# Second-part matmul groups in four single PSUM banks, and a LayerNorm finished for two tiles at a time, in a gated linear attention and gMLP kernel

## The chip, the cores and the metric

The kernel runs on one core of one Trainium2 chip. The metric is the device time of one execution in microseconds, and the kernel before and the changed one are compared by the medians of several executions. The core has five engines that run their own instruction streams side by side: TensorE (PE, with the loading of weights shown apart as PEld), VectorE (DVE), ScalarE (ACT), GpSimd (POOL) and SyncE (SP), whose queue issues the loads and stores. Matmuls write to PSUM, which has eight banks of 128 x 512 float32 values here; DVE and ACT carry results from there to SBUF.

## The reference

The first part is a recurrence over 768 tokens for 4 batches and 8 heads of 48, the second a gated MLP with a spatial mixing over the tokens:

```python
for t in range(S):
    state = alpha[:, :, t, :, None] * state + np.einsum('bhd,bhe->bhde', k[:, :, t], v[:, :, t])
    y[:, :, t] = np.einsum('bhd,bhde->bhe', q[:, :, t], state)
...
x = y.transpose(0, 2, 1, 3).reshape(B, S, H * D)            # 4 x 768 x 384
h = np.maximum(x @ w_in, 0.0)                               # d_ff = 1024
u, v = h[..., :512], h[..., 512:]
v_n = (v - mean(v)) / np.sqrt(var(v) + 1e-06)               # over the last axis
v_s = np.einsum('ts,bsd->btd', w_spatial, v_n) + b_spatial[None, :, None]
return (u * v_s) @ w_out                                    # 4 x 768 x 384, float32
```

## The kernel before, in words

The tokens are cut into tiles of 128: six per batch, 24 in all, numbered 0 to 23. `first(i)` lists the work on tile i of the recurrence in its chunked form: four loads (`ac`, `kc`, `qc`, `vc`: alpha, k, q and v, 192 KB each, on SP's queue), `ln` and the running sum `cum` (ACT, PE), the exponentials `einv`, `ebc`, `eexp` (ACT), the scaled `kt` (POOL) and `qt` (DVE), their transposes `trk` and `trq` (PE) and the copies out of PSUM `evk` and `evq` (ACT or DVE), the scores `sc` (PE), the masking `m` (DVE, tile `ptm`), the state's update `upd`, `z`, `S`, `sb` (PE, DVE, POOL), the output `y` (PE), and the transposition of `y` into `xT` of the batch (`xs`, `xt`, `xe`).

The second part works by batch. `second_v` multiplies `xT` by the second half of `w_in`, two tiles at a time, ACT applies the `relu` (line 139) and DVE takes the statistics (`bn`, lines 476 and 477). When all six tiles of a batch have theirs, `rs` makes `rstd` (two small ACT instructions, lines 486 and 487) and six `vn` normalise (DVE, line 493). `second_u` makes the other half, `second_s` the spatial product (six matmuls for each half `th` of the tokens) with its evacuation on DVE (line 541, and the product with `u` on POOL, line 553; in the last batch one DVE instruction, line 536). `second_o` multiplies by `w_out`, copies to `o_sb` and stores two tiles at a time (line 579). All these matmuls stand in the log under the helper's line 435.

`group` gives each of these steps one tile `ps2` of two PSUM banks out of a pool of two, so four banks in all. Two banks more serve `cum`, `tp` and `y`, and two hold `pt0` and `pt1`, each for a tile's transposes and then for its scores.

The order of each engine's instructions is not that of the listing. Every step is an `Op` with a planned duration, the steps it depends on, and a number `prio`; `schedule()` takes again and again the step that can start first by its plan, the lower `prio` where two can start at the same time, and emits it. The engines then run in that order and wait for each other by semaphores. A `Ring` stands for a pool of buffers in that plan.

Of the kernel before, what the change touches and what calls it, by code (L numbers as in the profile page):

```python
# [9 lines left out]
FP32 = mybir.dt.float32  # L10
# [6 lines left out]
class Op:  # L17


    def __init__(self, eng, dur, emit, deps=(), prio=0.0, take=None, give=(), lat=0.13):  # L20
        self.eng = {eng: dur} if isinstance(eng, str) else dict(eng)
        self.emit, self.prio, self.take, self.lat = emit, prio, take, lat
        self.deps = [d for d in deps if d is not None]
        self.give = list(give)
        self.end = None


class Ring:
# [5 lines left out]
    def free_at(self):  # L34
        n = len(self.taken) - self.bufs
# [13 lines left out]
def schedule(ops):  # L49
# [3 lines left out]
    while todo:  # L53
        best = None
        for n, op in enumerate(todo):
# [3 lines left out]
            if op.take is not None:  # L59
                f = op.take.ring.free_at()  # L60
                if f is None:
                    continue
                ready = max(ready, f)
# [12 lines left out]
        if op.take is not None:  # L76
            op.take.ring.taken.append(op.take)
# [6 lines left out]
def kernel(  # L84
# [26 lines left out]
    N = B * NCH  # L111

    consts = ctx.enter_context(tc.tile_pool(name="consts", bufs=1))
    IO = 7
# [30 lines left out]
    ident = consts.tile([128, 128], BF16, name="ident")  # L145
    mask4 = consts.tile([128, 4, 128], BF16, name="mask4")
# [11 lines left out]
    kt_bufs = [consts.tile([128, HP, 2, 64], BF16, name=f"kt{i}") for i in range(NB)]  # L158
    sbd_bufs = [consts.tile([128, HP, 2 * D], BF16, name=f"sbd{i}") for i in range(NB)]

    def constants(_):
        for t in la_bufs[:1] + qt_bufs[:1] + kt_bufs[:1] + sbd_bufs + la_bufs[1:] + qt_bufs[1:] + kt_bufs[1:]:
# [4 lines left out]
        nc.vector.memset(mask4, 0.0)  # L167
        nc.gpsimd.memset(ut_ones, 0.0)
# [9 lines left out]

    ops = []
# [15 lines left out]
    rings = {"a": Ring(2), "p0": Ring(1), "p1": Ring(1), "p2": Ring(2)}  # L195
# [4 lines left out]
    def first(i):  # L200
# [6 lines left out]
        def load(name, src):  # L207
            def emit(_):
                t = st[name] = io_pool.tile([128, H, D], FP32, name=name)
# [3 lines left out]
        for name, src, user in (("ac", alpha, "ln"), ("kc", k, "kt"), ("qc", q, "qt"), ("vc", v, "vb")):  # L213
            op((name, i), "SP", 1.11, load(name, src), got((user, i - IO)) + got(("order", i)), prio=P, lat=2.0)

# [11 lines left out]
        op(("ln", i), "ACT", 0.41, ln, got(("ac", i), ("cum", i - NB)), prio=P + 1)  # L227

        def cum(_):
            cm = st["cum"] = pp_a.tile([128, 512], FP32, name="cum", tag="a")  # L230
            nc.tensor.matmul(out=cm[:, 0:DM], lhsT=ut_ones, rhs=la[:, :, :, 0:D], start=True, stop=True)  # L231
            if not last:
                for hp in range(HP):
                    nc.tensor.matmul(  # L234
                        out=cm[:, DM + hp:DM + hp + 1], lhsT=la[:, hp, :, :], rhs=ones_col,
                        start=True, stop=True)

        sl_c = Slot(rings["a"])
        op(("cum", i), "PE", 0.16 if last else 0.3, cum, got(("ln", i)), prio=P + 2, take=sl_c)
# [8 lines left out]
        def eexp(_):  # L248
            nc.scalar.activation(out=st["cv"], in_=st["cv"], func=AF.Exp)  # L249

        op(("eexp", i), "ACT", 0.38, eexp, got(("einv", i)), prio=P + 3.1, use=[sl_c])
# [12 lines left out]
        def qtf(_):  # L264
            nc.vector.tensor_mul(out=qt[:, :, :, 0:D], in0=quad(st["qc"]), in1=st["cv"])  # L265
# [388 lines left out]
```

## Time and profile before

| what | us |
|---|---|
| median of 3 runs | 178.77 |
| lowest and highest | 178.15, 179.4 |
| the profiled execution | 177.04 |
| its span, first to last instruction | 175.3 |

The page begins with the share of each engine, and then the span in 40 slices of 4.4 us: each digit is the busy share of a slice in tenths, PEclk the clock that TensorE was granted in tenths of the full one.

```profile
PE 143.1 (82%) x1412; PEld 88.5 (50%) x1412; DVE 119.2 (68%) x257; ACT 98.0 (56%) x202; POOL 81.3 (46%) x134
## 2 busy tenths in 40 slices
PE   0562859838978999999978999999999899798960
PEld 0451536527545566655655666656565545343430
DVE  7374568763798489898899789998894467514400
ACT  4341567737796445789897664797874037300031
POOL 2641547642543569957823579985410770000000
PEclk9999999996995699999999999999999999999997
DMA  6999999999999999913979989869600001500033
```

The DMA engines are full for some 17 slices, PE from about the tenth slice on. A busy PE here is the union of its matmuls' durations, which overlap in the pipeline: a lone matmul of 384 columns lasts 0.34 us by its row, while 24 in a row take 4.06 us.

### The profile page before, as it was taken

How to read it: one execution, taken by the hardware profiler on the slowest of the kernel's cores; microseconds unless marked ns; L12 is line 12 of the kernel's file. 1: busy time of each engine (PE TensorE's matmuls, PEld its weight loads, DVE VectorE, ACT ScalarE, POOL GpSimd, SP SyncE). 2: the span in 40 equal slices, each digit the busy share in tenths (PEclk: the TensorE clock that was granted, in tenths of full speed). 3: DMA queues.
4: the chain of work that ended last, by engine and by line, in shares of the span. 5: the costliest groups of instructions: out<-in, count | busy, mean ns of one | idle time of the engine just before them, and what ended most of it. 6: DMA issues, size and time to landing. Idle time of an engine off the chain costs nothing.

```text
span 175.3 us, 3842 instructions
## 1 busy us (share of the span) xinstructions
PE 143.1 (82%) x1412; PEld 88.5 (50%) x1412; DVE 119.2 (68%) x257; ACT 98.0 (56%) x202; POOL 81.3 (46%) x134
## 2 busy tenths in 40 slices
PE   0562859838978999999978999999999899798960
PEld 0451536527545566655655666656565545343430
DVE  7374568763798489898899789998894467514400
ACT  4341567737796445789897664797874037300031
POOL 2641547642543569957823579985410770000000
PEclk9999999996995699999999999999999999999997
DMA  6999999999999999913979989869600001500033
GB/s 123 203 183 179 224 193 204 196 209 236 215 187 202 220 222 189 215 38 138 229 168 227 225 159 221 178 132 253 157 0 4 0 2 63 207 0 4 0 144 126
DMA packets 104947, 26.60 MB, mean 152 GB/s; under 512 B 100128, under 2 KB 104480, under 8 KB 104928
## 3 DMA queue, kind: packets, MB, share of 16 engines
q1 hardware_dynamic: 103104, 23.60, 63.7%
q0 software_dynamic: 1824, 2.75, 8.6%
q8 instruction: 11, 0.18, 0.4%
q14 instruction: 8, 0.07, 0.1%
HBM read 23.99 MB, written 4.72 MB: 164 GB/s over the span
## 4 chain that ended last, share of the span: by engine, by line
PE 46%; SPq 15%; DMA 13%; DVE 10%; ACT 10%; issue 3%; POOL 2%; ACTq 0%; POOLq 0%; DVEq 0%
PE ps L435 32%; SPq L210 15%; DMA ac<-in_alpha_dram 10%; PE pt L281 4%; DMA out_dram<-o_sb 3%; PE pt L344 2%; ACT o_sb L133 2%; DVE ptm L354 2%; PE y L390 2%; ACT v_sb L139 2%; DVE vsb L541 2%; DVE gT L536 2%; PE cum L231 2%; DVE stats L476 1%; PE tp L302 1%
## 5 line engine op out<-in xcount | busy, mean ns | idle before, releaser
L435 PE MATMUL ps<-w_spT,vn 128*128 128x384 bf16 x192 | 38.1, 338 | 1.0 <-DVE vsb L541 0.8
L354 DVE TENSOR_TENSOR ptm<-pt,mask 128x512 bf16<-128x512 f32 x48 | 30.8, 684 | 5.6 <-PE pt L344 5.1
L260 POOL TENSOR_TENSOR kt<-kc,binv 128x384 bf16<-128x384 f32 x24 | 21.9, 913 | 16.4 <-ACT bc L255 11.8
L553 POOL TENSOR_TENSOR gT<-vsb,uT 128x768 bf16<-128x768 f32 x12 | 19.6, 1642 | 13.0 <-DVE vsb L541 12.8
L435 PEld LDWEIGHTS <-vn 128*128 128x128 bf16 x192 | 17.6, 100 | 14.6 <-issue 5.9
L435 PE MATMUL ps<-xT,w_in_sb 128*128 128x384 bf16 x96 | 19.4, 326 | 2.7 <-ACT xT L133 1.0
L139 ACT ACTIVATE v_sb<-ps 128x1024 bf16<-128x1024 f32 x12 | 12.3, 1029 | 14.7 <-PE ps L435 14.6
L328 POOL TENSOR_TENSOR state<-state,bc 128x192 f32<-128x192 f32 x20 | 10.3, 513 | 21.7 <-DVE state L319 14.8
L133 ACT COPY o_sb<-ps 128x768 f32<-128x768 f32 x12 | 9.6, 806 | 18.8 <-PE ps L435 15.5
L435 PE MATMUL ps<-w_in_sb,xT 128*128 128x512 bf16 x72 | 19.1, 389 | 0.1
L265 DVE TENSOR_TENSOR qt<-qc,cum 128x384 bf16<-128x384 f32 x24 | 13.2, 549 | 8.4 <-ACT cum L249 4.8
L476 DVE BATCH_NORM_STATS2 stats<-v_sb 128x6 f32<-128x512 bf16 x24 | 16.3, 677 | 3.6 <-ACT v_sb L139 3.5
L225 ACT ACTIVATE la<-ac 128x384 bf16<-128x384 f32 x24 | 12.6, 524 | 10.7 <-DMA ac<-in_alpha_dram 10.7
L435 PE MATMUL ps<-w_out_sb,gT 128*128 128x384 bf16 x96 | 17.7, 325 | 0.8 <-DVE gT L536 0.3
L244 ACT ACTIVATE binv<-cum 128x384 bf16<-128x384 f32 x24 | 11.8, 492 | 11.7 <-PE cum L234 9.5
L133 ACT CAST x_sb<-y 128x384 bf16<-128x384 f32 x24 | 11.6, 483 | 7.7 <-PE y L371 7.7
L135 DVE COPY qkT<-pt 128x512 bf16<-128x512 bf16 x27 | 11.2, 421 | 6.7 <-PE pt L281 6.6
L271 POOL CAST vb<-vc 128x384 bf16<-128x384 f32 x24 | 12.1, 504 | 6.9 <-DMA vc<-in_v_dram 3.5
L231 PE MATMUL cum<-la,ut_ones 128*128 128x384 bf16 x24 | 8.6, 357 | 7.5 <-ACT la L225 6.8
L541 DVE TENSOR_TENSOR vsb<-ps,bsp_bc 128x768 f32<-128x768 f32 x12 | 11.4, 955 | 4.1 <-PE ps L435 3.9
L319 DVE TENSOR_TENSOR state<-tp,state 64x192 f32<-64x192 f32 x32 | 11.3, 353 | 3.6 <-PE tp L302 3.1
L133 ACT COPY qkT<-pt 128x512 bf16<-128x512 bf16 x21 | 12.4, 591 | 1.7 <-PE pt L281 1.6
(63 smaller groups left out, 243.7 us busy)
## 6 DMA issues: line engine op xcount, KB each, us to landing
ac<-in_alpha_dram SPq DMA_DIRECT2D x24, 192.0 KB, 3.8
kc<-in_k_dram SPq DMA_DIRECT2D x24, 192.0 KB, 3.9
qc<-in_q_dram SPq DMA_DIRECT2D x24, 192.0 KB, 3.7
vc<-in_v_dram SPq DMA_DIRECT2D x24, 192.0 KB, 3.7
out_dram<-o_sb SPq DMA_DIRECT2D x12, 384.0 KB, 2.5
wsp_nat<-in_moe_w_spatial_dram POOLq DMA_DIRECT2D x1, 1152.0 KB, 11.2
w_in_sb<-in_moe_w_in_dram POOLq DMA_DIRECT2D x1, 768.0 KB, 8.7
w_out_sb<-in_moe_w_out_dram POOLq DMA_DIRECT2D x1, 384.0 KB, 6.8
```

The lines of the kernel that those rows point to most:

```text
L133: nc.scalar.copy(out=out, in_=in_)
L139: nc.scalar.activation(out=out, in_=in_, func=AF.Relu)
L210: nc.sync.dma_start(out=t, in_=src[b, :, t0:t0 + C, :].rearrange("h s d -> s h d"))
L225: nc.scalar.activation(out=la[:, :, :, 0:D], in_=quad(st["ac"]), func=AF.Ln)
L231: nc.tensor.matmul(out=cm[:, 0:DM], lhsT=ut_ones, rhs=la[:, :, :, 0:D], start=True, stop=True)
L260: nc.gpsimd.tensor_mul(out=kt[:, :, :, 0:D], in0=quad(st["kc"]), in1=st["binv"])
L265: nc.vector.tensor_mul(out=qt[:, :, :, 0:D], in0=quad(st["qc"]), in1=st["cv"])
L354: nc.vector.tensor_tensor(out=st["ptm"][:, s], in0=st[f"pt{s}"], in1=mask4, op=ALU.mult)
L435: return lambda ps: nc.tensor.matmul(out=out(ps), lhsT=lhsT(), rhs=rhs(), start=start, stop=stop)
L476: nc.vector.bn_stats(out=stats, in_=d["v_sb"][:, tt, :])
L541: nc.vector.tensor_tensor(out=hold["vs"], in0=ps[:, :, 0:TH], in1=bsp_bc, op=ALU.add)
L553: nc.gpsimd.tensor_tensor(out=bt[b]["gT"][:, dsl, :].rearrange("p (a t) -> p a t", a=2), in0=hold["vs"], in1=bt[b]["uT"][:, dsl, :].rearra ...
```

## The change

Five things change, and the first two move the most instructions.

1. Second-part groups take one bank in place of two, from a pool of four (`pp_2`, ring `p2`). Each `v` group is now one tile, each `u` group one of four feature tiles, each `s` group one half of the tokens for one feature tile, each `o` group one tile. There are twice as many groups and evacuations, each of half the width; the matmuls are the same. `second_o` of a tile needs only the gated half that holds it, and `o_sb` has four buffers of half the size, with 24 stores in place of 12.
2. `second_ln` is gone: after every second tile, `second_v` lists `rs` and two `vn` for that pair. An `s` group comes in two pieces, the first with four token tiles and the second with two, and each waits only for its own `vn` (`pdeps`).
3. Every evacuation of a group gets `prio` 5.0 and every `rs` 6.0, so they precede all work of tiles 1 and later where both could start.
4. The scores no longer reuse the banks of the transposes: `pt` is one pool of two, from which each transposition and each half of the scores takes a bank when it needs it. `qkT` is split into `qT` and `kT`.
5. The loads of alpha and q get 4 buffers, those of k and v 6, where all had 7.

A second way to compute the first tiles (`fold`, with tokens interleaved in pairs) is in the code too, but `FOLD = 0` keeps it from being listed; only its constant tiles (`le_pair`, `lt_pair`, `le_tok`, and two alpha buffers) are filled at the start.

```diff
-    IO = 7
+    IO = 6
+    IO2 = 3
+    IO3 = 4
...
-    outp = ctx.enter_context(tc.tile_pool(name="outp", bufs=2))
+    outp = ctx.enter_context(tc.tile_pool(name="outp", bufs=4))
-    pp_p = ctx.enter_context(tc.tile_pool(name="pp_p", bufs=1, space=bass.MemoryType.PSUM))
-    pp_2 = ctx.enter_context(tc.tile_pool(name="pp_2", bufs=2, space=bass.MemoryType.PSUM))
+    pp_p = ctx.enter_context(tc.tile_pool(name="pp_p", bufs=2, space=bass.MemoryType.PSUM))
+    pp_2 = ctx.enter_context(tc.tile_pool(name="pp_2", bufs=4, space=bass.MemoryType.PSUM))
...
-        for t in la_bufs[:1] + qt_bufs[:1] + kt_bufs[:1] + sbd_bufs + la_bufs[1:] + qt_bufs[1:] + kt_bufs[1:]:
+        for t in la2_bufs[:1] + qt_bufs[:2] + kt_bufs + la2_bufs[1:] + sbd_bufs + qt_bufs[2:] + la_bufs:
             nc.vector.memset(t, 0.0)
...
+        nc.gpsimd.memset(le_tok, 0.0)
+        for ci in range(2):
+            nc.gpsimd.affine_select(
+                out=le_tok[64 * ci:64 * ci + 64], in_=le_tok[64 * ci:64 * ci + 64], compare_op=ALU.is_gt, fill=1.0,
+                base=0, channel_multiplier=2, pattern=[[1, 2], [-1, 128]],
+            )
+        for t, base in ((le_pair, 0), (lt_pair, 1)):
...
         nc.gpsimd.memset(ut_ones, 0.0)
...
-    rings = {"a": Ring(2), "p0": Ring(1), "p1": Ring(1), "p2": Ring(2)}
+    rings = {"a": Ring(2), "p": Ring(2), "p2": Ring(4)}
...
-        op(("sc", i), "PE", 0.4, sc, got(("evq", i), ("evk", i)), prio=P + 7, use=[sl0, sl1])
+        sl0, sl1 = Slot(rings["p"]), Slot(rings["p"])
+        qk = got(("evq", i0, 0), ("evq", i0, 1)) if fold else got(("evq", i))
+        op(("sc", i), "PE", 0.4, sc, qk + got(("evk", i)), prio=P + 7, take=[sl0, sl1])
...
-                    hold["ps"] = pp_2.tile([128, 2, 512], FP32, name="ps2")
+                    hold["ps"] = pp_2.tile([128, 512], FP32, name="ps2")
...
-        return op(key, eng, dur, lambda e: evac(e, hold["ps"]), [prev] + list(edeps), prio=prio, use=[sl])
+        return op(key, eng, dur, lambda e: evac(e, hold["ps"]), [prev] + list(edeps), prio=5.0, use=[sl])
...
-        op(("rs", b), "ACT", 0.45, rs, [made[("bn", b, t)] for t in range(NT)], prio=Q)
+        op(("rs", b, t0), "ACT", 0.45, rs, got(("bn", b, t0), ("bn", b, tt)), prio=6.0)
...
+        pdeps = [[made[x] for t in tt for x in (("vn", b, t), ("we", t))] for tt in ((0, 1, 2, 3), (4, 5))]
...
-        op(("st", b, tp), "SP", 1.11, store, got(("o", b, tp)), prio=-1.0, lat=2.0)
+            nc.sync.dma_start(out=out[b, tt * 128:(tt + 1) * 128, :], in_=hold["o"])
+        op(("st", b, tt), "SP", 0.56, store, got(("o", b, tt)), prio=-1.0, lat=2.0)
```

Three places show how the order moves. The first is where batch 0 ends and the scores of tile 7 are masked. On DVE before, between the masking of tile 6 and that of tile 7 (`ptm` with two score banks each):

```order
L354 TENSOR_TENSOR ptm<-pt_683,mask_87 128x512
L476 BN_STATS stats<-v_sb 128x6
L477 BN_AGGR mvs<-stats 128x2
L476 BN_STATS stats<-v_sb 128x6
L477 BN_AGGR mvs<-stats 128x2
L319 TENSOR_TENSOR state<-tp,state 64x192 x2
L493 TENSOR_SCALAR vn<-v_sb,mvs,rstd 128x512 x2
L354 TENSOR_TENSOR ptm<-pt_791,mask_87 128x512
L354 TENSOR_TENSOR ptm<-pt_811,mask_87 128x512
L493 TENSOR_SCALAR vn<-v_sb,mvs,rstd 128x512
L265 TENSOR_TENSOR qt_102<-qc,cum 128x8x48
L493 TENSOR_SCALAR vn<-v_sb,mvs,rstd 128x512 x3
```

The same place on DVE now:

```order
L477 TENSOR_TENSOR ptm<-pt,mask_90 128x512 x2
L594 BN_STATS stats<-v_sb 128x6
L595 BN_AGGR mvs<-stats 128x2
L144 TENSOR_SCALAR uT<-ps_869 128x384
L138 COPY kT<-pt 128x512
L438 TENSOR_TENSOR state<-tp,state 64x192
L612 TENSOR_SCALAR vn<-v_sb,mvs,rstd 128x512
L438 TENSOR_TENSOR state<-tp,state 64x192
L477 TENSOR_TENSOR ptm<-pt,mask_90 128x512 x2
L612 TENSOR_SCALAR vn<-v_sb,mvs,rstd 128x512
```

Two statistics and six `vn` around the masking have become one and two, and an evacuation of `u` and the copy of `kT` have come in. On PE before, from the last score of tile 7 to its `y` (rows left out are weight loads and repeats):

```order
L344 MATMUL pt_811<-qkT 128x128
...
L231 MATMUL cum<-la_99,ut_ones 128x384
...
L365 MATMUL y<-sbd_106,qkT 128x96
...
L371 MATMUL y<-vb,ptm 128x48
```

And on PE now:

```order
L465 MATMUL pt<-qT,kT 128x128
...
L513 MATMUL y<-ident,x_sb 128x128
...
L559 MATMUL ps_931<-w_spT,vn 128x384
...
L559 MATMUL ps_948<-w_spT,vn 128x384
...
L289 MATMUL cum<-la_102,ut_ones 128x384
...
L559 MATMUL ps_962<-w_spT,vn 128x384
...
L488 MATMUL y<-sbd_111,qT 128x96
...
L494 MATMUL y<-vb,ptm 128x48
```

Three pieces of the spatial product of batch 0 and a transposition of `x` now stand between the scores and `y`. The second place is the end, on ACT, from the last batch's first evacuations on. Before:

```order
L139 ACTIVATE uT<-ps_2547 128x2x384
L133 COPY o_sb<-ps_2558 128x768
L486 ACTIVATE rstd<-mvs,eps_tile 128x6
L487 ACTIVATE rstd<-rstd 128x6
L133 COPY o_sb<-ps_2574 128x768
L133 COPY o_sb<-ps_2589 128x768
L139 ACTIVATE uT<-ps_2617 128x2x384
L133 COPY o_sb<-ps_2697 128x768
L133 COPY o_sb<-ps_2702 128x768
L133 COPY o_sb<-ps_2718 128x768
```

Now:

```order
L142 ACTIVATE uT<-ps_2860 128x384
L142 ACTIVATE uT<-ps_2869 128x384
L605 ACTIVATE rstd<-mvs,eps_tile 128x2
L606 ACTIVATE rstd<-rstd 128x2
L136 COPY o_sb<-ps_2953 128x384
L136 COPY o_sb<-ps_2963 128x384
L136 COPY o_sb<-ps_2970 128x384
L136 COPY o_sb<-ps_2978 128x384
L136 COPY o_sb<-ps_2986 128x384
L136 COPY o_sb<-ps_2994 128x384
```

Copies of 384 columns stand where copies of 768 stood, and the last batch's `rstd` comes in three parts. The third place is SP's queue around the first stores. Before, where the loads of tile 15 begin:

```order
L210 DMA ac<-in_alpha_dram 128x8x48
L210 DMA kc<-in_k_dram 128x8x48
L579 DMA out_dram<-o_sb 128x2x384 x2
L210 DMA qc<-in_q_dram 128x8x48
L210 DMA vc<-in_v_dram 128x8x48
L210 DMA ac<-in_alpha_dram 128x8x48
L579 DMA out_dram<-o_sb 128x2x384
```

Now, where the loads of tile 12 begin:

```order
L231 DMA ac<-in_alpha_dram 128x8x48
L231 DMA kc<-in_k_dram 128x8x48
L684 DMA out_dram<-o_sb 128x384
L231 DMA qc<-in_q_dram 128x8x48
L231 DMA vc<-in_v_dram 128x8x48
L684 DMA out_dram<-o_sb 128x384 x2
L231 DMA ac<-in_alpha_dram 128x8x48
L684 DMA out_dram<-o_sb 128x384 x3
L231 DMA kc<-in_k_dram 128x8x48
```

The stores of batch 0 have moved three tiles ahead among the loads, and three of them stand between the alpha and the k of tile 13. The stores of batch 1, at tile 23 before, stand at tiles 19 and 20 now.

More of the change, by code (lines that the diff above doesn't have):

```diff
@@ L58, in schedule @@
             ready = max([d.end + d.lat for d in op.deps], default=0.0)
[L59 to L63, printed above, removed]
+            waits = [slot.ring.free_at(k) for k, slot in enumerate(op.take)]
+            if None in waits:
+                continue
+            ready = max([ready] + waits)
             for eng, dur in op.eng.items():
@@ L481, in second_ln, with bn @@
-    def second_ln(b):
-        Q = 1000.0 + 100 * b
+        group(("v", b, tt), mms, 0.22, got(("xe", b * NCH + tt), ("w_in",)), Q + tt, evac, {"ACT": 0.48}, None,
+              [made.get(("vn", b - 2, tt))], parts=1)
+        def bn(_):
+            d = bt[b]
+            stats = small.tile([128, 6], FP32, name="stats")
+            nc.vector.bn_stats(out=stats, in_=d["v_sb"][:, tt, :])
+            nc.vector.bn_aggr(out=d["mvs"][:, tt, :], in_=stats)
+        op(("bn", b, tt), "DVE", 0.85, bn, got(("v", b, tt)), prio=Q + 10)
@@ L575, in second_o @@
[L575 to L576 removed]
+            hold["o"] = outp.tile([128, DM], FP32, name="o_sb")
+            copy(eng, hold["o"], ps[:, 0:DM])
+        Q = 1000.0 + 100 * b + 30 + tt
+        group(("o", b, tt), mms, 0.165, [made[("g", b, x, tt // 3)] for x in range(NDS)] + got(("w_out",)), Q, evac,
+              {"ACT": 0.38, "DVE": 0.47}, None, [made.get(("st", b, tt - 4))], parts=1)
```

340 lines of the change are left out of this document (202 added, 138 removed).

## The prediction

> **What bounds the kernel now.** I read first the busy time by stage (columns: stretch, its length, then busy time and instructions of PE, PEld, DVE, ACT and POOL, then granted clock, DMA share and GB/s), then the chain of waits, then PE's own waits.
>
> ```profile
> 0.00:44.50 44.50, 26.43 (x304) 19.31 (x305) 27.52 (x67) 23.03 (x49) 20.96 (x43) 0.96 1.03 195
> 44.50:62.00 17.50, 15.27 (x154) 9.02 (x151) 13.32 (x31) 12.85 (x28) 7.76 (x15) 0.80 1.05 206
> 62.00:90.00 28.00, 27.30 (x317) 17.13 (x315) 24.70 (x53) 20.52 (x45) 20.54 (x31) 1.00 0.75 167
> 90.00:130.00 40.00, 37.85 (x432) 24.25 (x432) 35.80 (x78) 30.32 (x66) 25.58 (x41) 1.00 0.89 181
> 130.00:170.00 40.00, 36.24 (x217) 18.77 (x214) 17.83 (x32) 10.50 (x15) 6.49 (x4) 1.00 0.11 38
> ```
>
> ```profile
> 38.37 6.10 DMA ac<-in_alpha_dram
> ```
>
> Until 44.5 us the DMA engines are full (share 1.03) and PE works 26.4 of 44.5 us; the chain there ends in a load of alpha that lands at 44.5. The change moves the same bytes, so I let this stage stand: that alpha, of tile 7, lands at 44.5 in both kernels. Little second-part work can be pulled ahead of that moment, since it needs tiles that have not come; by the order, the new kernel has one group of three matmuls more behind it there.
>
> From 44.5 on PE is the bound (27.3 of 28.0, then 37.9 of 40.0 us). A gain there can only be PE time that is now waited for or run at a low clock. So the sum goes over PE's stands.
>
> **Term A, the LayerNorm of batch 0.** Before, all six `bn`, one `rs` and six `vn` of a batch come in one burst on DVE. The first fence is the timeline where it ends; the second gives windows (start and end, length, PE busy, instructions, granted clock, DMA share, GB/s).
>
> ```profile
> 50.71 0.93 DVE L493 TENSOR_SCALAR vn<-v_sb,mvs,rstd 128x512 bf16<-128x512 bf16 x2
> 51.67 1.29 DVE L354 TENSOR_TENSOR ptm<-pt,mask 128x512 bf16<-128x512 f32 x2
> 52.42 0.20 PE L371 MATMUL y<-vb,ptm 128*128 128x48 bf16 x1 [1.00 <-DVE ptm L354]
> 53.02 0.35 PE L371 MATMUL y<-vb,ptm 128*128 128x48 bf16 x7 [0.40 <-DVE ptm L354]
> 53.78 0.50 PE L281 MATMUL pt<-ident,kt 128*128 128x128 bf16 x3 [0.41 <-POOL kt L260]
> ```
>
> ```profile
> 36.00:38.00 2.00, 0.31 (x8) 1.00 1.25 238
> 40.00:42.00 2.00, 1.62 (x22) 0.50 1.16 308
> 52.00:54.00 2.00, 0.77 (x11) 0.82 0.72 139
> 54.00:60.00 6.00, 5.99 (x39) 0.50 1.10 218
> ```
>
> `y` of tile 7 needs the masked scores `ptm`; these stand on DVE behind two statistics and two `vn`. PE waits 1.00 + 0.40 + 0.41 = 1.8 us, and for the next 6 us its granted clock is 0.50: 6 x 0.5 = 3.0 us lost. After the change only `bn` of tile 5 and `vn` of tiles 4 and 5 are left at this place. DVE's row is not empty (an evacuation of `u` and of `k` now stand there too, some 1.3 us), so `ptm` is hardly earlier; what helps is PE's order. Three spatial matmul groups of batch 0 and the `x` transposes now stand between the scores and `y` of tile 7. Four tiles of vn are enough for them. These are some 2.3 us of PE work (the tail's full-clock rate is 0.163 us per matmul: 24 in 4.06 us, row below), which covers the 1.0 + 0.4 us. I take both parts: 1.8 and 3.0. Bounds: 0 and 1.8 for the wait, 0 or 3.0 for the clock.
>
> The earlier low clock (0.50 in 40 to 42) also came 2 to 4 us after a stretch in which PE did little (0.31 of 2.00 us). That supports tying the dip at 54 to the stand at 52. The Trainium skill (TensorE: Matmul & The Clock Gate, Part 1) says that the gate halves the clock after at least one idle window of about 3.4 us. The longest single stand here is 1.00 us, so by that rule the stand did not cause the dip, and the sum would be 172.8, the second case below. The trace agrees as to the two clocks, 1.00 and 0.50, and does not show the window's length.
>
> **Term B, the LayerNorm of batch 1.** The same burst, later:
>
> ```profile
> 91.74 0.65 PE L435 MATMUL ps<-xT,w_in_sb 128*128 128x384 bf16 x3 [0.77 <-ACT uT L139]
> 94.30 0.40 PE L281 MATMUL pt<-ident,qt 128*128 128x128 bf16 x4 [0.72 <-DVE qt L265]
> ```
>
> The first waits for a pair of banks to be emptied by one 768-wide `relu`, the second for DVE between two pieces of the `vn` burst. Both causes are split up by the change: 1.5 us, bounds 0 and 1.5.
>
> **Term C, the pairs of banks in the tail.** After tile 23 only second-part work is left, and PE waits for a pair to be emptied (the table of waits, 130 us to the end):
>
> ```profile
> PE ps L435 <- DVE gT L536: 1.1, 2, 0.8
> PE ps L435 <- ACT o_sb L133: 0.9, 2, 0.7
> PE ps L435 <- DVE vsb L541: 0.6, 1, 0.6
> PE ps L435 <- ACT uT L139: 0.4, 1, 0.4
> PE ps L435 <- ACT v_sb L139: 0.2, 1, 0.2
> ```
>
> Sum 3.2 us. With four single banks a group waits for the evacuation of the fourth group before it, which began some three groups of 0.5 to 0.65 us earlier and takes about 0.5 us. And `o` of the first three token tiles needs only the first half of the gated tile, so it no longer waits for the last `gT`. I take 3.2; lower bound 1.6, as an evacuation is half as wide.
>
> **Term D, the last stores.**
>
> ```profile
> 144.99 4.06 PE L435 MATMUL ps<-w_out_sb,gT 128*128 128x384 bf16 x24
> 168.28 1.46 PE L435 MATMUL ps<-w_out_sb,gT 128*128 128x384 bf16 x8 [0.28 <-ACT o_sb L133]
> 170.84 0.80 ACT L133 COPY o_sb<-ps 128x768 f32<-128x768 f32 x1 [1.91 <-DMA out_dram<-o_sb]
> DMA to landing us min/median/max: 2.4/2.5/4.1
> ```
>
> PE ends at 169.74 and the span at 175.3, 5.56 later; the last evacuation waits for a store to give back one of two buffers, ends at 171.64, and 3.66 us follow. After the change a tile of `o` costs PE four matmuls, 0.65 us, and its buffer is that of the fourth tile before. That tile leaves ACT about 4 x 0.65 - 0.5 = 2.1 us before PE ends; its store lands 2.5 us after issue, about 0.45 after PE ends; the last copy takes 0.5, then the same 3.66: 4.6 in place of 5.56. Gain 1.0. The last store is half as large; no row shows such a store and I give it nothing.
>
> **Term E, more and smaller instructions.** The rows of the evacuations and of the LayerNorm's two small activations:
>
> ```profile
> L139 ACT ACTIVATE v_sb<-ps 128x1024 bf16<-128x1024 f32 x12 | 12.3, 1029 | 14.7 <-PE ps L435 14.6
> L139 ACT ACTIVATE uT<-ps 128x768 bf16<-128x768 f32 x14 | 11.4, 811 | 2.9 <-PE ps L435 2.9
> L244 ACT ACTIVATE binv<-cum 128x384 bf16<-128x384 f32 x24 | 11.8, 492 | 11.7 <-PE cum L234 9.5 <-PE cum L231 2.1
> L486 ACT ACTIVATE rstd<-mvs,eps_tile 128x6 f32<-128x6 f32 x4 | 1.2, 309 | 0.3 <-DVE mvs L477 0.3
> L487 ACT ACTIVATE rstd<-rstd 128x6 f32<-128x6 f32 x4 | 0.8, 208 | 0.1
> L541 DVE TENSOR_TENSOR vsb<-ps,bsp_bc 128x768 f32<-128x768 f32 x12 | 11.4, 955 | 4.1 <-PE ps L435 3.9
> L265 DVE TENSOR_TENSOR qt<-qc,cum 128x384 bf16<-128x384 f32 x24 | 13.2, 549 | 8.4 <-ACT cum L249 4.8
> ```
>
> A 384-wide ACT instruction is 0.492 us, a 512-wide one by interpolation 0.60 (estimate). ACT gets 24 `v` for 12 (+2.1), 30 `u` for 14 (+3.4), 22 `o` for 12 (+1.1), 12 pairs of rstd for 4 (+4.1), less one weight copy of 0.8: about +10 us. DVE gets 32 spatial evacuations for 16, at 0.549 for 0.955: +2.3, and two small `o` copies. POOL's gating product is twice as many of half the width. In the tail and before 44.5 this hides: ACT is busy 10.5 of 40 us there, and at the start DMA rules. In 62 to 130 it meets an ACT that works 50.8 of 68 us and a DVE that works 60.5; about half of the additions (5.0 and 1.5 us) fall there. Bounds 0 and 6.5. I take 1.5: both engines keep slack, and outside the burst of term B PE hardly waits there.
>
> **What I cost at nothing.** The folded path is off (`FOLD = 0`), but its constants are built. POOL makes nine more instructions ahead of `ut_ones` and DVE fills the alpha buffers last, so the first tile starts 1 to 2.5 us later, and `w_in` lands about 1 us later while its first user stands earlier on PE. The cover is the DMA stage:
>
> ```profile
> 38.91 0.32 PE L231 MATMUL cum<-la,ut_ones 128*128 128x384 bf16 x1 [2.60 <-ACT la L225]
> ```
>
> PE stands 2.60 us here for alpha. If that cover fails the price is at most 2.5 us. The loads of alpha and q have 4 buffers in place of 7, and batch 0's stores stand in SP's queue between the loads of tiles 12 and 13, not at tile 15:
>
> ```profile
> 72.19 1.06 SPq L210 DMA_DIRECT2D kc<-in_k_dram  x1
> 80.25 1.79 SPq L579 DMA_DIRECT2D out_dram<-o_sb  x2
> ac<-in_alpha_dram SPq DMA_DIRECT2D x24, 192.0 KB, 3.8
> ```
>
> Even now SP stands 7.0 us behind a store at 73 while PE stays full. In the new order the load of k for tile 13 follows the last store of batch 0, and PE has then about 6 us of matmuls left before it transposes that k; the load takes 3.8 us to land and `kt` about 1 us more. I take 0. Bounds 0 and two stands of 3.8 us.
>
> **Sum.** 1.8 + 3.0 + 1.5 + 3.2 + 1.0 = 10.5, less 1.5 = 9.0 us. The profiled execution took 177.04 us (span 175.3 and 1.74 around it), and 177.04 - 9.0 = 168.0. It lies 1.7 us below the median of the runs shown, 178.77; I forecast a median, so 178.77 - 9.0 = 169.8.
>
> **The rivals and chances.** Slower or faster by over 1% means above 180.6 or below 177.0, about what a measurement of this kernel can tell.
>
> 1. Forecast, 169.8, chance 0.50; its own range 167 to 172.
> 2. The clock dip stays, since the stand at 52 is not its cause: 169.8 + 3.0 = 172.8. For it: the stands are short. Against: both dips follow a stretch of little PE work. 0.17.
> 3. Evacuations ahead of the first part. ACT takes ready evacuations (number 5) before the `Ln` and `Exp` of later tiles, and all 6.5 us of term E fall on the path in place of 1.5: 174.8; with one more dip like that at 54 (3.0), 177.8. For it: DVE is busy 35.8 of 40 us in 90 to 130. Against: PE waits little there now. 0.15, of which 0.07 above 177.
> 4. Slower: loads come late at both places where stores now stand ahead of them. Each costs one landing (3.8) and a dip after it (3.0): 13.6, so 183.4. It decides against the change from 10.8 us of stands on, that is, when PE reaches tiles 13 and 19 more than about 5 us before their k. For it: fewer buffers, earlier stores. Against: 7.0 us of SP's stand at 73 cost nothing. 0.09, of which 0.02 between 177 and 180.6.
> 5. More goes than I count: term E hides wholly and PE's remaining short stands close too: about 166. 0.09.
>
> Faster 0.50 + 0.17 + 0.09 + 0.08 = 0.84; same 0.07 + 0.02 = 0.09; slower 0.07. The range 165 to 176 leaves out the upper parts of cases 3 and 4 and a little of case 5, about 0.18.
>
> **What would show it.** Right: no PE wait at `y` of tile 7 and a granted clock near 1.0 from 44 to 62; no PE wait of more than 0.2 us on `ps` after tile 23; at most 4.8 us from the last matmul to the span's end; the landing of tile 7's alpha still near 44.5. Wrong: PE waits on `kt`, `qt` or `la` between tiles 12 and 20, a clock of 0.5 somewhere past 62, or SP's stands before loads of tiles 13 or 19 that end with PE idle.

## The result, and the profile after

The changed kernel took a median of 167.61 us (4 executions, 166.67 to 169.51) beside 178.46 us for the kernel before (4 executions, 176.05 to 179.4). The ratio is 0.945, with a 95% interval of 0.927 to 0.962. A second set with the same kernel gave 0.949 (0.941 to 0.957). Medians are of all executions; a ratio leaves out those more than 1.5% above the fastest of their kernel. The profiled execution is the slowest of its four: 169.51 us, span 167.7.

The busy time by stage of the kernel after (stretch, length, busy time and instructions of PE, PEld, DVE, ACT and POOL, granted clock, DMA share, GB/s):

```profile
0.00:44.50 44.50, 26.57 (x301) 19.10 (x305) 31.95 (x79) 23.37 (x54) 22.70 (x51) 1.00 1.03 194
44.50:62.00 17.50, 14.81 (x165) 9.42 (x165) 13.06 (x29) 10.85 (x27) 10.18 (x19) 0.90 0.94 184
62.00:90.00 28.00, 24.59 (x265) 15.13 (x265) 24.96 (x56) 20.97 (x54) 16.49 (x28) 1.00 0.86 188
90.00:130.00 40.00, 38.79 (x438) 25.05 (x440) 34.26 (x77) 32.78 (x83) 28.41 (x48) 1.00 0.84 177
130.00:163.00 33.00, 32.94 (x237) 18.04 (x236) 18.72 (x41) 15.65 (x37) 7.72 (x11) 1.00 0.13 45
```

The DMA stage is the same: share 1.03, PE 26.6 of 44.5 us. The stage from 130 us on has changed most: PE works 32.94 of 33 us, and it ends at 164.0 in place of 169.74. Between 62 and 90 us PE is now idle for 3.4 us by this trace, where it was idle for 0.7. The trace lacks the records of ten matmuls (62 of 72 by `w_in_sb` and `xT`); the second profile of the changed kernel, which lacks none, has 2.0 us of idle time there.

PE's timeline at `y` of tile 7, which waited 1.00 and 0.40 us before:

```profile
51.76 0.36 PE L494 MATMUL y<-vb,ptm 128*128 128x48 bf16 x8
51.97 0.38 PE L375 MATMUL pt<-ident,kt 128*128 128x128 bf16 x4
```

No row has an idle time behind it. But a little earlier there is a stand, and its clock is seen in three windows (PE busy and count, clock, DMA share, GB/s):

```profile
46.75 0.48 PE L289 MATMUL cum<-la,ut_ones 128*128 128x384 bf16 x1 [2.69 <-ACT la L268]
```

```profile
44.00:47.00 3.00, 0.31 (x3) 0.90 0.48 99
47.00:50.00 3.00, 2.78 (x22) 0.53 1.01 196
50.00:60.00 10.00, 9.86 (x116) 1.00 0.99 194
```

The running sum of tile 7 waits 2.69 us for that tile's alpha. Its load in the chain of waits (issue, and time to landing):

```profile
36.70 9.45 DMA ac<-in_alpha_dram
```

It lands at 46.15 here and landed at 44.5 before, though it is issued 1.7 us earlier than before (36.70 for 38.37). For the next 3 us the clock is 0.53. From 50 us on it is 1.00, where the kernel before ran at 0.50 from 54 to 60.

SP's queue at the stores of batch 0, and then the scores of tile 13: the last transposition ahead of them, the two copies on DVE that they need, and the scores on PE:

```profile
73.04 1.99 SPq L684 DMA_DIRECT2D out_dram<-o_sb  x3
75.12 1.74 SPq L231 DMA_DIRECT2D kc<-in_k_dram  x1
```

```profile
81.47 0.39 PE L375 MATMUL pt<-ident,qt 128*128 128x128 bf16 x4
87.50 0.39 DVE L138 COPY qT<-pt 128x512 bf16<-128x512 bf16 x1
87.81 0.41 DVE L138 COPY kT<-pt 128x512 bf16<-128x512 bf16 x1
88.28 0.40 PE L465 MATMUL pt<-qT,kT 48*128 48x128 bf16 x8 [1.60 <-DVE kT L138]
```

The scores do not wait for a load. The keys and queries of tile 13 have been transposed by 81.9 us, and the copies start 5.6 us later: from 80.8 us on DVE works without a listed wait, mostly on the statistics and `vn` of batch 1.

Last, the end, the landing time of the new stores, and the narrow evacuations (busy time and mean ns, then idle time):

```profile
160.59 3.41 PE L559 MATMUL ps<-w_out_sb,gT 128*128 128x384 bf16 x20
164.08 0.48 ACT L136 COPY o_sb<-ps 128x384 f32<-128x384 f32 x1 [0.17 <-PE ps L559]
```

```profile
L142 ACT ACTIVATE v_sb<-ps 128x512 bf16<-128x512 f32 x24 | 14.2, 595 | 6.0 <-PE ps L559 5.9
L142 ACT ACTIVATE uT<-ps 128x384 bf16<-128x384 f32 x30 | 13.6, 497 | 0.7 <-PE ps L559 0.7
L652 DVE TENSOR_TENSOR vsb<-ps,bsp_bc 128x384 f32<-128x384 f32 x24 | 13.2, 554 | 2.9 <-PE ps L559 2.4
out_dram<-o_sb SPq DMA_DIRECT2D x24, 192.0 KB, 2.0
```

The estimate of 0.60 us for a 512-wide evacuation on ACT was right (595 ns). The last copy starts 0.08 us after the last matmul, and the span ends 3.7 us after it (5.56 before). The table of PE's waits from 130 us to the end is empty.

### The profile page after: what moved, and what is told of

It reads as the page before. It is cut to its first block, busy times and chain, and to the rows that moved or that the text cites. A ratio compares the mean times of both kernels' runs of the same rounds, so it can differ in the third digit from the quotient of the medians.

```text
span 167.7 us, 3952 instructions
## 1 busy us (share of the span) xinstructions
PE 138.7 (83%) x1402; PEld 87.1 (52%) x1412; DVE 123.0 (73%) x278; ACT 104.8 (62%) x255; POOL 85.5 (51%) x155
## 4 chain that ended last, share of the span: by engine, by line
PE 55%; DMA 13%; DVE 10%; ACT 9%; POOL 6%; issue 4%; DVEq 0%; POOLq 0%; ACTq 0%
PE ps L559 36%; DMA ac<-in_alpha_dram 6%; PE pt L375 5%; DMA w_in_sb<-in_moe_w_in_dram 5%; PE pt L465 3%; POOL kt L322 3%; PE y L513 3%; PE cum L289 2%; DMA qc<-in_q_dram 2%; PE tp L421 2%; DVE ptm L477 2%; ACT uT L142 2%; PE y L488 2%; DVE vn L612 2%; PE y L494 2%
## 5 line engine op out<-in xcount | busy, mean ns | idle before, releaser
L664 POOL TENSOR_TENSOR gT<-vsb,uT 128x384 bf16<-128x384 f32 x24 | 21.6, 912 | 2.3 <-DVE vsb L652 2.2
L559 PEld LDWEIGHTS <-vn 128*128 128x128 bf16 x192 | 16.4, 97 | 9.4 <-issue 1.4
L136 ACT COPY o_sb<-ps 128x384 f32<-128x384 f32 x22 | 10.5, 482 | 16.6 <-PE ps L559 16.1
L559 PE MATMUL ps<-w_in_sb,xT 128*128 128x512 bf16 x62 | 18.1, 407 | 2.7 <-DMA w_in_sb<-in_moe_w_in_dram 1.8
L559 PE MATMUL ps<-xT,w_in_sb 128*128 128x384 bf16 x96 | 18.9, 328 | 0.7 <-ACT v_sb L142 0.7
L142 ACT ACTIVATE v_sb<-ps 128x512 bf16<-128x512 f32 x24 | 14.2, 595 | 6.0 <-PE ps L559 5.9
L652 DVE TENSOR_TENSOR vsb<-ps,bsp_bc 128x384 f32<-128x384 f32 x24 | 13.2, 554 | 2.9 <-PE ps L559 2.4
L375 PE MATMUL pt<-ident,kt 128*128 128x128 bf16 x96 | 10.2, 234 | 4.8 <-POOL kt L322 4.2
L142 ACT ACTIVATE uT<-ps 128x384 bf16<-128x384 f32 x30 | 13.6, 497 | 0.7 <-PE ps L559 0.7
```

What stands on the lines that cost most here:

```text
L136: nc.scalar.copy(out=out, in_=in_)
L142: nc.scalar.activation(out=out, in_=in_, func=AF.Relu)
L375: nc.tensor.transpose(hold["t"][:, hp, :], src[:, hp, :, :], ident)
L559: return lambda ps: nc.tensor.matmul(out=out(ps), lhsT=lhsT(), rhs=rhs(), start=start, stop=stop)
L652: nc.vector.tensor_tensor(out=hold["vs"], in0=ps[:, 0:TH], in1=bsp_bc[:, th, :], op=ALU.add)
L664: nc.gpsimd.tensor_tensor(out=bt[b]["gT"][:, dsl, cols], in0=hold["vs"], in1=bt[b]["uT"][:, dsl, cols], op=ALU.mult)
```

## The experiments

Ratios are to the kernel before, run beside each set on the same chip; the interval is 95%. Line numbers shift by a few in kernels with added or removed lines.

### First set: the changed kernel again, and three parts of it undone

> The changed kernel once more, as the yardstick of this set. All theories: 166 to 169.5 us, ratio to the kernel before 0.93 to 0.96. In its profile no wait of PE on ps after tile 23, and a wait of 1 to 2 us of PE for kT near the scores of tile 13.

Measured: 168.98 us, ratio 0.949 (0.941 to 0.957). In this profile the wait for tile 7's logarithm was 2.95 us, and the dip behind it is twice as long:

```profile
47.00:53.00 6.00, 5.49 (x30) 0.51 0.95 181
```

So far do two executions of one kernel differ before 54 us. The wait at the scores of tile 13 is 0.49 us, less than the 1 to 2 that were expected.

LayerNorm once per batch, everything else as changed:

```diff
-        if tt % 2 == 0:
+        if tt < NT - 1:
             return
...
-            r = d["rstd"][:, t0:t0 + 2]
+            r = d["rstd"]
...
-        for t in (t0, tt):
+        for t in range(NT):
```

> The changed kernel with the LayerNorm finished once for six tiles, all else as changed. If terms A and B of the prediction come from the LayerNorm in pairs, most of 1.8 + 3.0 + 1.5 = 6.3 us is lost: 172 to 174 us, with PE waits at y of tile 7 or before the spatial product of batches 0 and 1. If instead the single banks and the new order of PE bring them (the spatial pieces between scores and y), it stays at 167 to 170.

Measured: 167.5 us, ratio 0.945 (0.939 to 0.950). Not slower than the changed kernel. PE at `y` of tile 7 in this kernel:

```profile
51.19 0.37 PE L494 MATMUL y<-vb,ptm 128*128 128x48 bf16 x8
```

The stand is gone with all six tiles of a batch normalised in one piece. So the finish per pair is not needed for it. Another of 1.02 us comes 4.5 us later, for a step of the state on DVE, and no dip of the clock follows it. What is left of the change (single banks, four groups deep, and the order that follows from them) is enough.

The order numbers back to the batch's own:

```diff
-        ... [prev] + list(edeps), prio=5.0, use=[sl])
+        ... [prev] + list(edeps), prio=prio, use=[sl])
-        op(("rs", b, t0), ..., prio=6.0)
+        op(("rs", b, t0), ..., prio=Q)
```

> The changed kernel with the numbers of the evacuations and of rs set back to those of their batch, so the first part goes ahead of them. If evacuations ahead of the first part cost PE time (the third case of the prediction), it is faster by 1.5 to 5 us: 163 to 166. If they only order what is hidden anyway: 167 to 169. If the four single banks live on quick evacuations: 170 or more, with PE waits on ps.

Measured: 169.74 us, ratio 0.953 (0.945 to 0.961). That is 0.4% above the changed kernel of the same set, with intervals that overlap: no worth of the order numbers is shown, and the third case of the prediction (they cost PE time) is not borne out.

The constants of the unused folded path left out, and the buffers zeroed in the old sequence:

```diff
-        nc.gpsimd.memset(le_tok, 0.0)
-        for ci in range(2):
-            nc.gpsimd.affine_select(
...
```

> The changed kernel without the constants of the unused folded path and with the fills in the order of before. The prediction put their price at nothing, under cover of the loads: 167 to 168.5 us, with the first cum 0.9 us earlier and tile 7's alpha where it was. If the start counts: 165 to 166.5.

Measured: 170.55 us, ratio 0.953 (0.946 to 0.961). No gain is seen, though the first `cum` runs 0.87 us earlier (4.22 for 5.09). The price of nothing that the prediction put on these constants stands.

### Second set: parts of the change added to the kernel before

LayerNorm per pair alone, with the pairs of banks kept:

```diff
+            r = d["rstd"][:, t0:t0 + 2]
...
-        op(("rs", b), "ACT", 0.45, rs, [made[("bn", b, t)] for t in range(NT)], prio=Q)
-        for t in range(NT):
+        op(("rs", b, t2), "ACT", 0.45, rs, got(("bn", b, t0), ("bn", b, t0 + 1)), prio=Q)
+        for t in (t0, t0 + 1):
...
-        second_ln(b)
```

> The kernel before with one part of the change: rstd and the two normalisations are listed per pair of tiles; pairs of banks, order numbers and loads are as before. Theory 1 (terms A and B of the prediction): the burst of six on DVE is what held up y of tile 7 and the two waits of batch 1, so 1.8 + 3.0 + 1.5 = up to 6.3 us go and the ratio is near 0.965, with a clock of 1.0 at 54 to 60. Theory 2 (after the changed kernel with LayerNorm per batch was no slower): the stands went because single banks let other matmuls stand ahead of y on PE; LayerNorm per pair by itself gives under 1.5 us, ratio 0.99 to 1.00, and a stand at y of tile 7 or at a neighbour stays.

Measured: 176.24 us, ratio 0.990 (0.982 to 0.997), near theory 2. The stand at `y` of tile 7 did go, and the clock is 1.00 from 50 to 66 us, as theory 1 has it. But PE now waits at other places between 36 and 64 us (the table of waits):

```profile
PE y L390 <- ACT x_sb L133: 1.3, 3, 0.5
PE ps L446 <- ACT w_spT L133: 1.1, 1, 1.1
```

What the clock gains there it loses earlier: the dip that lasts from 39.6 to 43.0 us in the kernel before lasts from 41.8 to 48.6 in this one. The burst was a cause of that stand, but taking it away alone is worth 1%.

Matmuls put into the stand: the kernel before with the sum of tile 8 multiplied nine times over.

```diff
-            nc.tensor.matmul(out=cm[:, 0:DM], lhsT=ut_ones, rhs=la[:, :, :, 0:D], start=True, stop=True)
+            for _ in range(9 if i == 8 else 1):
+                nc.tensor.matmul(out=cm[:, 0:DM], lhsT=ut_ones, rhs=la[:, :, :, 0:D], start=True, stop=True)
```

> The kernel before in which the running sum of tile 8, which stands on PE ahead of y of tile 7, is multiplied nine times over into the same bank (the result is that of one): eight more matmuls of about 0.16 to 0.34 us, 1.3 to 2.7 us of PE work, in the place of the stands of 1.00 and 0.40 us. Theory 1: the stands at 52 to 54 us cause the clock of 0.50 at 54 to 60; with PE kept busy the clock stays near 1.0 there, 3.0 us come back less up to 1.3 us that the added matmuls outlast the stands: ratio 0.985 to 0.995. Theory 2: the dip has another cause (the work of the engines before it, or time by itself): the clock still falls to 0.50 for some 6 us within 50 to 66, and the time is that of before or up to 1.5 us more: ratio 1.00 to 1.01.

Measured: 175.49 us, ratio 0.986 (0.979 to 0.993). More matmuls, and less time. A window of the kernel before at that stand, then PE's timeline and windows in this one:

```profile
51.00:54.00 3.00, 1.18 (x20) 0.88 0.81 157
```

```profile
53.09 0.35 PE L372 MATMUL y<-vb,ptm 128*128 128x48 bf16 x7 [0.31 <-DVE ptm L355]
54.20 0.40 PE L282 MATMUL pt<-ident,kt 128*128 128x128 bf16 x4 [0.76 <-POOL kt L261]
```

```profile
51.00:54.00 3.00, 2.13 (x25) 1.00 0.78 150
54.00:60.00 6.00, 5.64 (x70) 1.00 1.05 208
```

The clock stays at 1.00 from 54 to 60 us: in these profiles the dip goes with the lack of PE work around 52 us. The next kernel, whose order is that of the kernel before, has the stand and the dip again, 3 us later. How much of the 1.4% is the clock stays open, because the earlier dip is longer in this profile (37.9 to 44.7 us), and the mean clock over whole executions moved little: 0.972 to 0.974 in the four that the ratio uses, 0.957 to 0.976 in the seven of the kernel before that stand beside them.

Four buffers for `o_sb` in the kernel before:

```diff
-    outp = ctx.enter_context(tc.tile_pool(name="outp", bufs=2))
+    outp = ctx.enter_context(tc.tile_pool(name="outp", bufs=4))
```

> The kernel before with four buffers for o_sb in place of two, in the same order. Theory 1 (term D): the last copy no longer waits 1.91 us for a store to give its buffer back, so the end from the last matmul to the span's end falls from 5.56 to about 3.7 to 4.6 us, and the time by 1.0 to 1.9 us: ratio 0.989 to 0.995. Theory 2: the store's 3.66 us and the queue decide; the end stays at 5.0 to 5.6 us, ratio 0.997 to 1.00.

Measured: 177.14 us, ratio 0.988 (0.978 to 0.998). Its windows at the repeated stand, and its end:

```profile
54.00:57.00 3.00, 1.17 (x20) 0.96 0.77 152
57.00:60.00 3.00, 2.99 (x26) 0.50 1.04 205
```

```profile
169.81 1.46 PE L435 MATMUL ps<-w_out_sb,gT 128*128 128x384 bf16 x8 [0.24 <-ACT o_sb L133]
171.35 0.80 ACT L133 COPY o_sb<-ps 128x768 f32<-128x768 f32 x1 [0.89 <-ACT o_sb L133]
```

The last copy no longer waits for a store. PE ends at 171.27 and the span at 175.8, 4.53 us later in place of 5.56. So 1.03 us of the end are the buffers, as term D had it.

Seven buffers for every load in the changed kernel:

```diff
-                t = st[name] = io_pool.tile([128, H, D], FP32, name=name, bufs=bufs)
+                t = st[name] = io_pool.tile([128, H, D], FP32, name=name, bufs=7)
```

> The changed kernel with seven buffers again for every load (alpha and q have 4 in it, k and v 6), in the same order. Theory 1 (the prediction costed this at nothing): loads come as late as their place in the queue behind the stores, not for want of a buffer; the time is that of the changed kernel, ratio 0.940 to 0.953, and the scores of tile 13 still wait 1 to 2 us. Theory 2: four buffers hold alpha and q back from about 44 us on; seven bring up to 3.8 us, ratio 0.925 to 0.935, and alpha of tile 7 lands at 44.5 or sooner in place of 46.

Measured: 167.19 us, ratio 0.944 (0.936 to 0.951). No cost of the smaller rings is seen. In this profile the sum of tile 7 ran at 45.36, and again after a wait of 2.69 us; the scores of tile 13 waited 0.49 us, not the 1 to 2 of theory 1.

### Third set: depth of banks, the stand for tile 7, the stores, and all together

Two single banks in place of four:

```diff
-    pp_2 = ctx.enter_context(tc.tile_pool(name="pp_2", bufs=4, space=bass.MemoryType.PSUM))
+    pp_2 = ctx.enter_context(tc.tile_pool(name="pp_2", bufs=2, space=bass.MemoryType.PSUM))
-    rings = {"a": Ring(2), "p": Ring(2), "p2": Ring(4)}
+    rings = {"a": Ring(2), "p": Ring(2), "p2": Ring(2)}
```

> The changed kernel with two single banks for second-part groups in place of four, in the pool and in the planner's ring; everything else, the width of the groups among it, as changed. Theory 1 (term C: the depth of four groups takes away the waits for banks): PE again waits for evacuations in the tail, 3 us or more after tile 23, and has fewer groups to pull ahead of y in the middle; 4 to 8 us of the gain go, ratio 0.965 to 0.99. Theory 2 (half the width is what helps, since an evacuation is done sooner): the waits in the tail stay under 1.5 us, ratio 0.945 to 0.96.

Measured: 177.32 us (12 executions), ratio 0.982 (0.973 to 0.992). Two thirds of the gain are gone. Only three of the 12 executions enter the ratio; the medians of all give 0.988. PE's windows from 44.5 us to its last matmul:

```profile
44.50:62.00 17.50, 15.35 (x181) 1.00 0.99 194
...
90.00:130.00 40.00, 36.32 (x423) 1.00 0.79 167
130.00:168.63 38.63, 37.32 (x233) 1.00 0.13 47
```

The time is in the range of theory 1, but the place is not the tail, where it expected 3 us of waits or more: the listed waits after 130 us add up to 0.9 us, as theory 2 had it, and most of PE's idle time lies before. From 90 to 130 us it is 40 - 36.32 = 3.7 us, half of it in two waits for an evacuation of `u` (the table of waits of that stretch):

```profile
PE ps L559 <- ACT uT L142: 1.9, 2, 1.6
```

The tail is also longer: from `y` of tile 23 to PE's last matmul it takes 168.63 - 134.96 = 33.7 us, in the changed kernel 164.0 - 137.68 = 26.3, and in the kernel before 38.2. With four groups open PE does more of the second part between the pieces of the first. This run halves the PSUM space of the groups together with their number; no run separates the two.

Twelve matmuls in the stand for tile 7, in the changed kernel:

```diff
+                for _ in range(12 if i == 7 else 0):
+                    nc.tensor.matmul(out=cm[:, 0:DM], lhsT=ut_ones, rhs=la_bufs[(i - 1) % NB][:, :, :, 0:D], start=True, stop=True)
                 nc.tensor.matmul(out=cm[:, 0:DM], lhsT=ut_ones, rhs=la[:, :, :, 0:D], start=True, stop=True)
```

> The changed kernel, in which twelve matmuls on the logarithms of tile 6 are put ahead of the running sum of tile 7, in the same bank (the sum overwrites them): about 0.33 + 11 x 0.163 = 2.1 us of PE work in the place where PE has stood 2.7 to 4.0 us for the logarithm of tile 7 in every profile of the changed kernel and its variants, and after which its clock was 0.50 to 0.6 for 3 to 6 us. Theory 1 (a short stand is enough to lower the clock): the clock stays near 1.0 behind it, 1.5 to 3 us come back, ratio 0.927 to 0.937. Theory 2 (the dip comes from the longer stretch of little work between 36 and 47 us, or from something else): the dip stays or moves, ratio 0.943 to 0.953.

Measured: 167.59 us, ratio 0.947 (0.938 to 0.955). The windows of its profile, of the tail and of the place in question:

```profile
130.00:159.54 29.54, 29.49 (x193) 1.00 0.17 61
```

```profile
44.00:47.00 3.00, 2.39 (x25) 1.00 1.08 211
47.00:50.00 3.00, 3.00 (x35) 1.00 1.06 208
```

The dip is gone, as theory 1 has it, and from the sum of tile 7 to PE's last matmul 159.54 - 45.19 = 114.35 us pass, where the changed kernel took 164.0 - 46.75 = 117.25. The times of whole executions show no gain: the profiled one, 165.12 us, is the quickest of its six, and their median is that of the changed kernel. That is not because the dip came back. Three of the six had a mean clock of 0.998 to 1.00 and took 167.19 to 167.72 us; the six of the changed kernel with seven buffers took 166.89 to 169.23, and three of these 167.01 to 167.24 at a clock of 0.965 to 0.979. So a full clock by itself did not make the execution shorter. What takes the gain back is not shown; the added matmuls alone are 2.1 us of work.

Stores of batches 0 and 1 behind later loads:

```diff
+                if name == "vc" and i in (14, 21):
+                    while late:
+                        late.pop(0)()
...
-            nc.sync.dma_start(out=out[b, tt * 128:(tt + 1) * 128, :], in_=hold["o"])
+            late.append(lambda: nc.sync.dma_start(out=out[b, tt * 128:(tt + 1) * 128, :], in_=hold["o"]))
+            if b > 1:
+                late.pop()()
```

> The changed kernel with the stores of batch 0 issued behind the loads of tile 14 and those of batch 1 behind the loads of tile 21, and six buffers for o_sb; the order on the other engines is the same. Theory 1: the stores ahead of the loads of tile 13 cause the wait of PE for that tile's keys (0.5 to 1.6 us in the profiles) and its neighbours; 0.5 to 2 us come back, ratio 0.933 to 0.945. Theory 2: PE is the bound there and what it waits less at 13 it waits elsewhere; ratio 0.943 to 0.953, as the changed kernel.

Measured: 167.43 us, ratio 0.941 (0.931 to 0.951). The interval holds both theories. The wait at the scores of tile 13 is 0.5 us here, as in several kernels with the early stores (0.5 in the changed kernel's second profile, 1.6 in its first). That fits a wait for DVE, whose copy of `kT` runs late here too (88.69 us). No cost of the stores is shown.

All four edits together: the twelve matmuls, the late stores, seven buffers for each load, and no constants for the folded path.

> All four together on the changed kernel: the twelve added matmuls ahead of the running sum of tile 7, late stores, seven buffers for every load, and no constants for the folded path. If the gains add up as theory 1 has it for each: 2 to 5 us less than the changed kernel, ratio 0.915 to 0.935. If PE's work from 44 us on is the whole bound and the first 44 us are set by the loads: 0.940 to 0.950.

Measured: 166.66 us, ratio 0.937 (0.928 to 0.947), the lowest median of all. It cannot be told from the changed kernel with certainty: 0.937 lies outside that kernel's interval in the second measurement and inside it in the first.

## Why the prediction was right, and where it was not

The forecast was 169.8 us with a range of 165 to 176; 167.61 came out. The sum was 9.0 us; the two profiled executions differ by 7.5 us and the medians by 10.9. What follows splits each profile from 44.5 us to PE's last matmul into three parts, worked out from the windows by stage: PE time lost to a low clock (length times one minus the clock), PE idle, and the rest, PE busy at full clock.

| kernel | busy at full clock | lost to the clock | idle | sum, us | last matmul to end |
|---|---|---|---|---|---|
| before | 113.2 | 3.5 | 8.6 | 125.2 | 5.6 |
| before, stand filled | 115.4 | 0.2 | 7.7 | 123.3 | 5.5 |
| two single banks | 113.9 | 0.0 | 10.3 | 124.1 | 3.8 |
| changed | 110.4 | 1.8 | 7.4 | 119.5 | 3.7 |
| changed, stand filled | 111.1 | 0.0 | 4.0 | 115.0 | 3.8 |

In the second row the early dip ends at 44.7 us, so that its loss falls ahead of the cut.

**Term A, the wait: right in size, the cause half right.** The 1.8 us are gone. The prediction named two causes, the burst of LayerNorm on DVE and PE's order. Each can remove the stand: LayerNorm per pair did in the kernel before, and single banks did with LayerNorm per batch. In the changed kernel the pairs are not needed.

**Term A, the clock: mechanism right, gain given back.** The dip at 54 to 60 is gone, and filling the stand with matmuls in the kernel before removes it too, so the second case (the stand is not its cause) finds no support. The fourteen profiles together say the same: they have 25 dips past 20 us, and ahead of each, ending at most 1.25 us before it, lies a stretch of 3 us in which PE worked 1.6 us or less, in 24 of them 1.35 or less. In the kernel before the clock halved at 53.3 us, when PE had worked 1.6 of the last 3; with the stand filled, the least 3 us of work there hold 1.8, and it did not. The Trainium skill (TensorE: Matmul & The Clock Gate, Part 1) gives at least one idle window of about 3.4 us as the condition. No window here was wholly idle, so the measurement decides: a stretch of 3 us with PE at work for 1.6 was enough. What the prediction missed is the next stand: it asked for a clock near 1.0 from 44 to 62, and the sum of tile 7 waits 2.69 us for alpha, so that the clock falls there instead: 1.8 us in one profile, 3.5 by the same sum in the other (windows 0.51 from 47 to 53). So the net gain of this term is 0 to 1.7 us of clock (3.5 less one or the other) in place of 3.0, and the changed kernel with its stand filled shows that clock won need not be time won.

**Term B: the two waits went, others came.** The waits of 0.77 and 0.72 us at 91.7 and 94.3 have gone, and idle PE time from 90 to 130 us went from 2.15 to 1.21 us. But batch 1's LayerNorm still makes PE wait, earlier: 0.66 us at 85.06 for a `relu` and 1.60 at 88.28 for copies behind it on DVE (0.56 and 0.49 in the second profile).

**Term C: right in size.** The windows from 130 us to the last matmul, of the kernel before and of the changed one:

```profile
130.00:169.74 39.74, 36.23 (x217) 1.00 0.10 36
```

```profile
130.00:164.00 34.00, 33.94 (x242) 1.00 0.15 53
```

PE's idle time there went from 3.5 us to 0.06, where 3.2 was predicted. The depth of four is a part of it: with two banks PE idles 1.3 us there. LayerNorm per pair is perhaps another, since by itself it brought the kernel before to 1.9 us there. How the rest divides is not shown.

**Term D: too small.** 1.9 us in place of 1.0. The buffers give 1.03, as the kernel before with four of them shows. The other 0.8 belong to the last piece of half the size; of the store's half the prediction had said that no row shows it, and given it nothing: the copy takes 0.48 us in place of 0.80, and a store of 192 KB lands in 2.0 us where one of twice the size took 2.5.

**Term E: the sum holds, the place was not foreseen.** ACT is busy 6.8 us more over the whole run (104.8 for 98.0), not 10, and 2.9 more between 62 and 130. PE's idle time in that stretch holds the gain of B and the price of E together, 1.5 less 1.5 in the prediction. It went from 2.85 us to 4.62 in the first profile, whose trace lacks ten matmuls, to 3.05 in the second and to 3.1 in the one with the stand filled, which lacks ten too: 0.2 to 1.8 us more for a predicted 0. So E cost about what B brought, or up to 1.8 us more. Its largest wait is the one for DVE at tile 13, where the prediction looked for a late load. That is close to a sign that it had named as wrong (PE waiting on `kt` or `qt` between tiles 12 and 20), for another reason.

**Not in the sum: shorter busy time.** By the table PE's busy time at full clock fell by about 2.8 us. Most of that comes from the cut at 44.5 us. Busy time multiplied by the clock, in windows of 1 us over the whole span, adds up to 138.3 us before and to 137.3 and 137.2 in the two profiles of the changed kernel (138.8 with two banks). The difference is about 1 us; the rest was done earlier, 24.4 us of work up to 44 us before, 26.5 and 25.4 now. No run tested where the 1 us went, and some matmul records are missing from several traces.

**Costed at nothing.** No run shows a price of the constants, the smaller rings or the stores ahead of loads. The landing of tile 7's alpha was not near 44.5, as the prediction's last part asked: the sum that follows it ran at 45.19 to 47.83 us where its order was the changed kernel's. With the order of the kernel before it ran at 45.06 to 46.70. The two overlap, and the spread of the DMA stage is a part of the spread of the times; a mean about 1 us later (46.8 over seven profiles, 45.6 over three) may be the change's, which no run settles. A candidate is a difference that the list of the change leaves out: the load of the spatial weights (1152 KB) follows `vb` of tile 3 in place of `kt`. It was issued at 27.0 to 28.9 us in those seven profiles and at 26.4 to 26.6 in the three, and in the changed kernel's first profile it landed at 40.9 in place of 37.8. No run takes this difference back.

**Which part brings the gain.** By ratios: LayerNorm per pair alone 0.990; all of the change with two banks 0.982; all of it with four 0.945 to 0.949; the same without LayerNorm per pair 0.945; without the order numbers 0.953. Four single banks rather than two bring about two thirds, and the rest is not split further (the spatial groups are also listed half by half of the tokens now, which no run undoes). That the sum came so near is in part luck: the wait of A and the tail of C were sized rightly, and D was 0.9 too small, but B and E came out near each other through waits that were not foreseen, the clock's 3.0 were too much, and about 1 us of shorter busy time and the work done earlier were not in it.

## What to carry to other kernels

Where one engine is the bound and fills PSUM for others to empty, look at how many groups can be open at once rather than at the width of one: the whole change with the same banks cut into four single groups gave 5% here, and with two single banks only 2%. Filling a stand of PE with matmuls that change nothing tells whether a dip of the clock belongs to it; whether the dip costs time is to be read from the times, not from the clock. After removing one stand, look for the next stretch of little work, since it can take over the dip. And where an engine waits, look at what the releasing engine was doing before blaming a load.

## What the runs showed of the hardware

The clock fell to 0.50 after stretches that were far from idle (PE busy 1.6 of the last 3 us in the kernel before, at 53.3, and 1.2 in the one with four `o_sb` buffers, at 56.8). In windows of 0.25 us, the 25 dips past 20 us in the fourteen profiles last either 3.25 to 3.5 us or 6.75 to 7.0, nothing between. The clock did not fall after every stand. Of 27 stretches of 3 us past 20 us with PE at work for 1.25 us or less, 22 had a dip that started in their last part or up to 1.1 us behind them, and five had none. One of the five holds 2.38 us without a matmul, from 38.5 to 40.9 in the changed kernel:

```profile
40.90 1.51 PE L570 MATMUL ps<-ident,wsp_nat 128*128 128x128 bf16 x24 [2.38 <-DMA wsp_nat<-in_moe_w_spatial_dram]
```

```profile
40.00:42.00 2.00, 1.10 (x20) 1.00 1.23 285
```

So the length of a stand alone does not tell whether a dip follows; where the stand lies may matter, and these runs do not settle it.
